# Attention and feed-forward in one kernel: later adding transfers for the second batch, and a new plan that keeps VectorE's two-operand SBUF work behind GpSimd's queue

## The chip, the core and the metric

The kernel runs on one core of a Trainium2 chip. A core has TensorE (PE, matmuls), VectorE (DVE), ScalarE (ACT), GpSimd (POOL) and SyncE (SP, which issues most transfers). Each engine works through its own list of instructions in order, and semaphores tie the lists together. The metric is device time in microseconds (us), the median of several runs.

## The reference, cut to what matters

```python
B, C, H, W = 4, 128, 384, 32          # q: (4, 12288, 128), kv: (4, 384, 32, 128)
kv_pool = kv.reshape(B, H // 4, 4, W // 4, 4, C).mean(axis=(2, 4))   # 768 keys for each batch
k = v = kv_pool.reshape(B, -1, C) @ w_sr
s = (q @ k.transpose(0, 2, 1)) / sqrt(C)
a = exp(s - s.max(-1)); a /= a.sum(-1) + 1e-09
x = (a @ v).reshape(4 * 12288, C)
h = x @ w_in                           # w_in: (128, 2048)
out = (h - tanh(h)) @ w_out            # w_out: (2048, 128)
```

## The kernel before, in words

The 49,152 tokens are cut into 96 groups of 512, 24 for each batch. A group has an attention part and a feed-forward part, and both use expansions about a mean instead of the exact functions. The attention part makes three score tiles of 128x1024 (`big`, L1063), a ScalarE function of them (`p`, L1067), their square on GpSimd (`r2`, shown as r, L1070), a sum over values on TensorE (`x`, L1113), and some 128x512 steps on the side: `qr` (L1048), `m` (L1091), `ql` (L1107) and `dr` (L1120) on GpSimd, `dy` (L1103) and `dl` (L1117) on VectorE. The feed-forward part makes eight hidden tiles (`big`, L1170), squares them on ScalarE (`u`, L1174), forms a cubic term on VectorE (`r`, L1177, a ring of four buffers), multiplies it back into one PSUM bank (`acc`, L1189), and VectorE adds a column and writes the result `o` (L1200).

Before the groups of a batch can run, its keys and weights have to be made. For the first batch this is the prologue. SP loads w_in in four pieces (L412), the first batch's kv in twelve (L566), then w_out in four (L414). `words_of` turns each piece of a weight matrix into float32: two ScalarE steps (L430, L446), three VectorE steps (L433, L436, L440), and a last VectorE step `add` (L449), which adds two SBUF operands. VectorE sums eight of the kv pieces (L580) and GpSimd folds the other four (L574). TensorE turns w_in (L476), multiplies it with itself (L495), and makes keys and values (L644, L632, L649, L677). From the w_in pieces and the centre of the keys come `first` (L756), a chain of small VectorE operations (`first_chain`), and then the batch's own weights: `winr` (L928 and L935) and `Wr` (`by_third`, L970, on GpSimd, one for each quarter, which reads that quarter of w_out). TensorE sums `Wg` against each quarter of w_out into the bank `acc` (`slopes`, L957), and a short chain (L966, L989, L992, L996, L999) ends in the tables that every group of the batch needs. Since `acc` is one bank, no group can begin its sum in it before this chain is over.

Each later batch is pooled by transfers: SP issues a first one (L535), and GpSimd then issues seven that add into the same tile `kvp` (L533), each behind the landing of the one before; `join` adds the two halves.

What sets the order: nothing is written in program order. Each piece of work is a `plan.op` with a step (its place), an engine, a cost, a delay after it (`late`) and, for two-operand VectorE work in SBUF, `port=True`. `Plan.run` walks these with a simple model of the engines, of one port that GpSimd and such VectorE work share, and of the transfer queues. At each turn it takes, on each engine, the lowest step among what can begin soon, and then the engine that begins first. The instructions are emitted in that order. The table MOVES shifts the steps of named pieces; from the fourth group on, each group's steps are the same. BUFS gives the buffers of each ring.

Of the kernel before, what the change touches and what calls it, by code (L numbers as in the profile page):

```python
# [46 lines left out]
class Plan:  # L47
# [36 lines left out]
    def run(self, between):  # L84
# [67 lines left out]
        while True:  # L152
            best = None
            for e, q in ready.items():
                if q:
                    starts = []
                    for r, i in q:
                        held = free.get("port", 0.0) if self.ops[i][5] else 0.0
                        starts.append((max(free.get(e, 0.0), r, held), self.ops[i][0], i, r))
                    soon = min(starts)[0] + self.SOON  # L160
                    step, i, start, r = min((p, i, t, r) for t, p, i, r in starts if t <= soon)
                    if best is None or (start, step, i) < best[:3]:
                        best = start, step, i, e, r
            done = landed(best[0] if best else math.inf)
# [37 lines left out]
def attention_then_ffn(ctx: ExitStack, tc: tile.TileContext, q, kv_by_key, kv_by_place, w_sr, w_in,  # L202
# [17 lines left out]
    plan = Plan(tc)  # L220

    MOVES = {
# [1269 lines left out]
```

## Time and profile before

| | |
|---|---|
| median of 3 runs | 1270.63 us (1270.61 to 1271.1) |
| the profiled execution: time, span | 1270.95 us, 1269.2 us |
| mean granted TensorE clock | 0.988 |
| TensorE busy | 1217.5 us (96%) |
| VectorE, ScalarE, GpSimd busy | 1153.5, 1143.2, 1057.7 us |

The span runs from the first to the last instruction of the profiled execution; the time holds a little more around it. A granted clock of 1.0 is 2.4 GHz, 0.5 is 1.2 GHz. In the rows of a timeline the first number is the start in us from the span's start, the second the length, and the brackets at the end give the idle time of that engine just before and who ended it. Records of neighbouring instructions on one engine can overlap a little.

### The profile page before, as it was taken

What the parts mean: (1) busy time and instruction counts of PE and PEld (TensorE: products, weight loads), DVE (VectorE), ACT (ScalarE), POOL (GpSimd) and SP (SyncE); (2) the same over time, 40 slices, a digit from 0 to 9 for tenths busy, and PEclk for the clock granted to TensorE, in tenths of its full rate; (3) what the DMA queues carried; (4) which work ended last, traced back from release to release, by engine and by line L of the source; (5) the groups of instructions that cost most, each with busy time, mean ns of one, the idle gap of its engine ahead of it and who ended that gap; (6) DMA issues with size and microseconds to landing.
All of it is one profiled execution on the core that took longest, in us unless ns stands there. A gap on an engine that the chain in (4) does not pass through costs nothing.

```text
span 1269.2 us, 16667 instructions
## 1 busy us (share of the span) xinstructions
PE 1217.5 (96%) x5252; PEld 936.1 (74%) x5252; DVE 1153.5 (91%) x1218; ACT 1143.2 (90%) x1373; POOL 1057.7 (83%) x836
## 2 busy tenths in 40 slices
PE   5779999999999999999999999999999999999997
PEld 5656777777777777767777777777777777777775
DVE  6768999999999999998999999998899999999997
ACT  3658999999999999989999999999999999999994
POOL 5668888799999888789999888789988887888881
PEclk9879999999999999999999999999999999999998
DMA  9444111121453111111464111111111111111101
GB/s 358 100 83 92 51 42 42 43 84 59 93 119 89 50 42 42 42 46 56 113 122 106 42 51 42 42 43 59 51 51 42 43 50 42 42 42 51 34 26 35
DMA packets 41713, 84.49 MB, mean 67 GB/s; under 512 B 5040, under 2 KB 7216, under 8 KB 41616
## 3 DMA queue, kind: packets, MB, share of 16 engines
q1 hardware_dynamic: 35904, 66.82, 15.7%
q0 software_dynamic: 5712, 16.52, 7.7%
q8 instruction: 44, 0.72, 0.2%
q14 instruction: 53, 0.43, 0.1%
HBM read 57.93 MB, written 25.39 MB: 66 GB/s over the span
## 4 chain that ended last, share of the span: by engine, by line
PE 84%; DVE 5%; ACT 3%; POOL 2%; issue 2%; DMA 2%; SPq 0%; ACTq 0%; DVEq 0%
PE big L1170 27%; PE acc L1189 25%; PE big L1063 10%; PE x L1113 9%; PE acc L1156 5%; DVE r L1177 3%; PE x L1085 2%; ACT u L1174 2%; PE x L1094 2%; PE acc L1160 2%; PE x L957 1%; ACT p L1067 1%; DMA Wr<-in_kv_by_key_dram 1%; DMA r<-in_kv_by_key_dram 1%; POOL r L1070 1%
## 5 line engine op out<-in xcount | busy, mean ns | idle before, releaser
L1177 DVE SCALAR_TENSOR_TENSOR r<-big,u 128x1024 fp32r<-128x1024 f32 x768 | 902.2, 1219 | 86.4 <-ACT u L1174 64.9
L1174 ACT ACTIVATE u<-big 128x1024 f32<-128x1024 f32 x768 | 762.2, 1028 | 48.5 <-PE big L1170 44.7
L1070 POOL TENSOR_TENSOR r<-p 128x1024 fp32r<-128x1024 f32 x288 | 556.7, 1936 | 111.3 <-ACT p L1067 111.1
L1170 PE MATMUL big<-dr,winr 128*128 128x512 f32 x1536 | 488.1, 407 | 4.2 <-ACT p L1067 2.3
L1189 PE MATMUL acc<-r,Wr 128*128 128x512 f32 x1536 | 454.2, 396 | 2.1 <-DVE o L1200 1.8
L1170 PEld LDWEIGHTS big<-dr,winr 128*128 128x128 f32 x1536 | 271.1, 189 | 105.3 <-DVE r L1177 29.9
L1189 PEld LDWEIGHTS acc<-r,Wr 128*128 128x128 f32 x1536 | 289.0, 189 | 68.9 <-DVE o L1200 2.2
L1067 ACT ACTIVATE p<-big 128x1024 f32<-128x1024 f32 x288 | 296.6, 1030 | 18.9 <-PE big L1063 5.3
L1063 PE MATMUL big<-qr,kTr 128*128 128x512 f32 x576 | 186.8, 406 | 1.5 <-ACT p L1067 0.7
L1113 PE MATMUL x<-r,vvr 128*128 128x512 f32 x576 | 165.0, 394 | 0.2 <-DVE dy L1103 0.2
L1120 POOL TENSOR_TENSOR dr<-dl,yk 128x512 fp32r<-128x512 f32 x96 | 129.3, 1347 | 41.9 <-DVE dl L1117 41.8
L1063 PEld LDWEIGHTS big<-qr,kTr 128*128 128x128 f32 x576 | 101.4, 189 | 41.3 <-ACT p L1067 21.6
L1091 POOL TENSOR_TENSOR m<-yk,q 128x512 fp32r<-128x512 f32 x96 | 129.9, 1353 | 0.0
L1107 POOL TENSOR_TENSOR ql<-q,qr 128x512 fp32r<-128x512 f32 x96 | 129.7, 1352 | 0.0
L1113 PEld LDWEIGHTS x<-r,vvr 128*128 128x128 f32 x576 | 107.5, 188 | 25.4 <-DVE dy L1103 0.9
L1200 DVE TENSOR_SCALAR o<-acc,At 128x512 f32<-128x512 f32 x96 | 71.3, 743 | 1.6 <-PE acc L1160 1.5
L1103 DVE SCALAR_TENSOR_TENSOR dy<-x,yk 128x512 f32<-128x512 f32 x96 | 65.4, 681 | 4.2 <-ACT t L1097 4.2
L1088 ACT ACTIVATE yk<-x 128x512 f32<-128x512 f32 x96 | 58.0, 604 | 10.7 <-PE x L1085 9.4
L1117 DVE TENSOR_TENSOR dl<-x,dy 128x512 fp32r<-128x512 f32 x96 | 65.4, 682 | 1.1 <-PE x L1113 0.4
L1048 POOL TENSOR_SCALAR qr<-q 128x512 fp32r<-128x512 f32 x96 | 62.2, 647 | 1.0 <-DMA q<-in_q_dram 0.9
L1156 PE MATMUL acc<-qr,Lh 128*128 128x512 f32 x192 | 60.5, 397 | 1.5 <-DVE o L1200 1.5
L1097 ACT ACTIVATE t<-x 128x512 f32<-128x512 f32 x96 | 57.9, 603 | 2.0 <-PE x L1094 2.0
(195 smaller groups left out, 640.7 us busy)
## 6 DMA issues: line engine op xcount, KB each, us to landing
q<-in_q_dram SPq DMA_DIRECT2D x96, 256.0 KB
out_dram<-o SPq DMA_DIRECT2D x96, 256.0 KB
kvp<-in_kv_by_place_dram POOLq DMA_DIRECT2D x21, 768.0 KB, 7.2
kc<-inverse SPq DMA_DIRECT2D x12, 256.0 KB
kvp<-in_kv_by_place_dram SPq DMA_DIRECT2D x3, 768.0 KB
winr<-in_kv_by_key_dram SPq DMA_DIRECT2D x4, 512.0 KB
r<-in_kv_by_key_dram SPq DMA_DIRECT2D x4, 512.0 KB
Wr<-in_kv_by_key_dram SPq DMA_DIRECT2D x4, 512.0 KB
```

Of the source, the lines that this page charges most:

```text
L1063: PE.matmul(out=half(plan[s], h), lhsT=plan[kTr][:, n * P : (n + 1) * P], rhs=plan[qr], start=True, stop=True)
L1067: A.activation(out=plan[p], in_=plan[s], func=AF.Silu, scale=1.0 / 3)
L1070: PL.tensor_tensor(out=plan[r], in0=plan[p], in1=plan[p], op=ALU.mult)
L1091: PL.tensor_tensor(out=plan[m], in0=plan[yk], in1=plan[qs], op=ALU.mult)
L1107: PL.tensor_tensor(out=plan[ql], in0=plan[qs], in1=plan[qr].bitcast(F32), op=ALU.subtract)
L1113: PE.matmul(out=plan[num], lhsT=plan[vvr][:, n], rhs=half(plan[f"r2.{g}.{k}"], h), start=(start and h == 0), stop=(stop and h == 1))
L1120: PL.tensor_tensor(out=plan[dr], in0=plan[dl].bitcast(F32), in1=plan[yk], op=ALU.add)
L1156: PE.matmul(out=plan[acc], lhsT=x, rhs=plan[y], start=(start and n == 0), stop=(stop and n == 2))
L1170: PE.matmul(out=half(plan[hp], h), lhsT=plan[winr][:, f * P : (f + 1) * P], rhs=plan[dr], start=True, stop=True)
L1174: A.activation(out=plan[u], in_=plan[hp], func=AF.Square)
L1177: V.scalar_tensor_tensor(out=plan[r], in0=plan[hp], scalar=1.0, in1=plan[u], op0=ALU.add, op1=ALU.mult)
L1189: PE.matmul(out=plan[acc], lhsT=plan[Wr][:, 2 * n + h], rhs=half(plan[r], h), start=(start and h == 0), stop=(stop and h == 1))
```

## The change

Four things are edited. The planner gets a rule: when the next piece would be a VectorE operation that needs the port, begins just as the port comes free, and GpSimd has a queued operation that could begin at most 0.12 later, GpSimd's is taken first. The second batch's first pooling transfer (L535) is given a `late` of 30 in the model, so that the adding transfers behind it are planned later. Two other numbers of the model change (`late` of the w_out loads, cost of `first_chain`). And all of MOVES is replaced; its rows tell a reader nothing, and one line of it stands here.

```diff
         while True:
-            best = None
+            best = pool = None
...
+                    if e == "POOL":
+                        pool = start, step, i, e, r
                     if best is None or (start, step, i) < best[:3]:
                         best = start, step, i, e, r
+            if (best and pool and best[3] != "POOL" and self.ops[best[2]][5] and not self.ops[pool[2]][6]
+                    and pool[0] <= best[0] + 0.12 and 0 < free.get("port", 0.0) <= best[0]
+                    and best[0] <= free["port"] + 1e-9):
+                best = pool
...
-        "load.i.0": -3373.262, "words.i.0": -3532.267, "load.i.1": -881.918, "words.i.1": -947.206,
+        "load.i.0": -4159.973, "words.i.0": -2510.035, "load.i.1": -4127.904, "words.i.1":
...
-        plan.op(load_step, "SP", 0.5, load_words, (), (own,), late=2.0 if kind == "i" else 4.5, dma=1.3)
+        plan.op(load_step, "SP", 0.5, load_words, (), (own,), late=2.0 if kind == "i" else 5.5, dma=1.3)
...
-                    late=0.81 if w else 1.0, dma=5.84 if w else 2.2)
+                    late=0.81 if w else 30.0 if b == 1 else 1.0, dma=5.84 if w else 2.2)
...
-            plan.op(known, on, 3.7, first_chain, ((prep, "h"),), ((prep, "t"), (hb, 8), iv, ("stat", b)))
+            plan.op(known, on, 3.4, first_chain, ((prep, "h"),), ((prep, "t"), (hb, 8), iv, ("stat", b)))
```

No instruction is added or taken away; what the chip sees is another order on each engine. Lines of the changed kernel are eight higher. On SP the fourth w_in piece is loaded ahead of all kv pieces. On VectorE five sums of kv pieces stand ahead of the last two `add` of w_in, where two stood, and three of the four w_out pieces are finished before `first_chain`, where one was. The order changes in the prologue, around the second batch's tables, and in a few places of the third and fourth batch.

The first place is GpSimd around the four `Wr` of the first batch (the last three and the first three of a row stand here). Before:

```order
L970 TENSOR_TENSOR Wr<-wout_69,hb 128x512
L1120 TENSOR_TENSOR dr<-dl,yk 128x512
L1070 TENSOR_TENSOR r_570<-p 128x1024
L1091 TENSOR_TENSOR m<-yk,q 128x512
L1070 TENSOR_TENSOR r_576<-p 128x1024
L970 TENSOR_TENSOR Wr<-wout_69,hb 128x512
L533 DMA kvp<-in_kv_by_place_dram 128x2x768
L1003 TENSOR_TENSOR Lh<-L_595,Lh 128x128
```

And in the changed kernel:

```order
L1078 TENSOR_TENSOR r_435<-p 128x1024
L1099 TENSOR_TENSOR m<-yk,q 128x512
L1128 TENSOR_TENSOR dr<-dl,yk 128x512
L978 TENSOR_TENSOR Wr<-wout_69,hb 128x512 x4
L1078 TENSOR_TENSOR r_547<-p 128x1024
L1011 TENSOR_TENSOR Lh<-L_540,Lh 128x128
```

Four operations stood between the third and the fourth `Wr`; now the four stand together, and the adding transfers (L533, now L541) come after all of this.

The second place is TensorE around the last of the four `slopes` (L957, now L965) and the chain behind it. Before:

```order
L1170 MATMUL big<-dr,winr 128x512 x2
L957 MATMUL acc<-Wg,wout_69 128x129 x4
L989 MATMUL acc<-ident,At 128x128
L996 MATMUL acc<-A,Mn 128x128
L1160 MATMUL acc<-dl,Ah 128x512
L1189 MATMUL acc<-r,Wr 128x512 x6
```

And in the changed kernel:

```order
L1178 MATMUL big<-dr,winr 128x512 x6
L516 MATMUL x<-Mn 128x128
L965 MATMUL acc<-Wg,wout_69 128x129 x4
L1121 MATMUL x<-r_435,vvr 128x512 x2
L997 MATMUL acc<-ident,At 128x128
L1071 MATMUL big<-qr,kTr 128x512 x2
L1178 MATMUL big<-dr,winr 128x512 x2
L1004 MATMUL acc<-A,Mn 128x128
L1178 MATMUL big<-dr,winr 128x512 x2
L1071 MATMUL big<-qr,kTr 128x512 x2
L1121 MATMUL x<-r_547,vvr 128x512 x2
L1168 MATMUL acc<-dl,Ah 128x512
```

Three of the first group's eight hidden tiles stand ahead of the last `slopes`, where seven stood, and the steps of the chain have other matmuls between them.

The third place is TensorE up to the first score tiles (L1063, now L1071). Before:

```order
L632 MATMUL big<-kvp,wsr 128x384
L644 MATMUL big<-wsr,kvp 128x128
L623 MATMUL x<-row,wsr 128x1
L644 MATMUL big<-wsr,kvp 128x128
L649 MATMUL big<-wsr,row 128x128 x3
L756 MATMUL acc<-col,win_67 128x64 x4
L649 MATMUL big<-wsr,row 128x128 x3
L756 MATMUL acc<-col,win_67 128x64 x4
L1063 MATMUL big<-qr,kTr 128x512 x2
L677 MATMUL x<-kc 128x128 x6
```

And in the changed kernel:

```order
L764 MATMUL acc<-col,win_67 128x64 x4
L652 MATMUL big<-wsr,kvp 128x128 x2
L657 MATMUL big<-wsr,row 128x128 x6
L640 MATMUL big<-kvp,wsr 128x384
L764 MATMUL acc<-col,win_67 128x64 x8
L685 MATMUL x<-kc 128x128 x6
L1071 MATMUL big<-qr,kTr 128x512 x2
```

The first scores now stand behind a third `first` (L756, now L764) and the moment of the values (L677, now L685).

## Rows read from the trace of the kernel before

**Rows 1.** The page: busy time of each engine, and TensorE's by slices.

```profile
PE 1217.5 (96%) x5252; PEld 936.1 (74%) x5252; DVE 1153.5 (91%) x1218; ACT 1143.2 (90%) x1373; POOL 1057.7 (83%) x836
PE   5779999999999999999999999999999999999997
```

**Rows 2.** Windows: length, busy us and counts by engine, granted clock, DMA share, GB/s.

```profile
37.30:41.90 4.60, 0.01 (x1) 0.01 (x1) 2.20 (x14) 2.61 (x4) 4.60 (x4) 0.81 0.58 86
41.90:47.00 5.10, 5.10 (x17) 4.30 (x18) 3.12 (x10) 2.38 (x6) 4.22 (x3) 0.50 0.54 128
47.00:65.40 18.40, 15.57 (x83) 11.07 (x81) 14.62 (x21) 10.78 (x15) 13.65 (x11) 1.00 0.36 62
65.40:71.80 6.40, 0.01 (x1) 0.01 (x1) 6.33 (x1) 1.69 (x2) 5.78 (x4) 0.66 0.59 112
71.80:81.10 9.30, 8.22 (x23) 6.16 (x24) 2.79 (x3) 1.67 (x6) 3.68 (x4) 0.50 0.50 85
81.10:98.20 17.10, 13.36 (x54) 9.43 (x52) 11.95 (x12) 13.18 (x15) 8.81 (x7) 1.00 0.44 80
98.20:101.60 3.40, 3.14 (x8) 2.50 (x9) 1.33 (x2) 0.60 (x1) 3.20 (x3) 0.50 0.74 142
...
155.20:190.50 35.30, 35.30 (x152) 27.39 (x151) 33.55 (x34) 34.26 (x40) 30.03 (x22) 1.00 0.14 45
```

**Rows 3.** Timeline around the last `add` of w_out, VectorE, GpSimd and TensorE.

```profile
52.60 0.68 DVE L449 CUSTOM_DVE_ANT_0 wout<-wout,o 128x1024 uint16<-128x1024 uint16 x1
...
64.57 1.71 POOL L1120 TENSOR_TENSOR dr<-dl,yk 128x512 fp32r<-128x512 f32 x1
...
65.15 6.58 DVE L449 CUSTOM_DVE_ANT_0 wout<-wout,o 128x1024 uint16<-128x1024 uint16 x1
65.80 2.31 POOL L1070 TENSOR_TENSOR r<-p 128x1024 fp32r<-128x1024 f32 x1
...
68.88 2.30 POOL L1070 TENSOR_TENSOR r<-p 128x1024 fp32r<-128x1024 f32 x1
...
71.79 2.09 PE L957 MATMUL acc<-Wg,wout 128*128 128x129 f32 x8 [6.41 <-DVE wout L449]
```

**Rows 4.** Timeline of what followed on VectorE and TensorE.

```profile
78.31 4.82 DVE L1177 SCALAR_TENSOR_TENSOR r<-big,u 128x1024 fp32r<-128x1024 f32 x4 [6.57 <-PE acc L1189]
...
88.40 0.74 PE L1156 MATMUL acc<-qr,Lh 128*128 128x512 f32 x2 [1.53 <-DVE o L1200]
...
98.46 0.77 PE L1085 MATMUL x<-qr,Mh 128*128 128x512 f32 x1 [2.22 <-DVE dl L1117]
```

**Rows 5.** Timeline of the prologue up to the first group's shares.

```profile
17.87 3.78 PE L476 MATMUL big<-ident,win 128*128 128x128 f32 x16 [3.39 <-DVE win L449]
18.87 1.21 DVE L580 TENSOR_REDUCE kvp<-winr 128x64 f32<-128x1024 f32 x1
...
32.03 0.71 PE L1063 MATMUL big<-qr,kTr 128*128 128x512 f32 x2
...
32.58 1.50 PE L677 MATMUL x<-kc 128*128 128x128 f32 x12
...
34.39 1.00 PE L756 MATMUL acc<-col,win 128*128 128x64 f32 x8
...
41.89 0.80 PE L1094 MATMUL x<-m,share 128*128 128x512 f32 x1 [4.63 <-POOL m L1091]
```

**Rows 6.** Timeline of VectorE: results of the eighth, ninth and tenth group.

```profile
178.75 0.74 DVE L1200 TENSOR_SCALAR o<-acc,At 128x512 f32<-128x512 f32 x1
...
190.55 0.74 DVE L1200 TENSOR_SCALAR o<-acc,At 128x512 f32<-128x512 f32 x1
...
204.11 0.74 DVE L1200 TENSOR_SCALAR o<-acc,At 128x512 f32<-128x512 f32 x1
```

**Rows 7.** An adding transfer on GpSimd, and a later window in which three begin.

```profile
337.82 1.21 POOL L533 DMA_DIRECT2D kvp<-in_kv_by_place_dram  x1
...
360.00:400.00 40.00, 40.00 (x172) 30.85 (x171) 38.06 (x38) 38.88 (x47) 39.07 (x31) 1.00 0.59 119
```

196 rows, old and new, of the table MOVES are left out of this document.

## The prediction

> **What bounds the kernel now.** I read the page first. TensorE is busy for 96% of the span, and its slices read 9 from the fourth on but for the last; only the first three are low [rows 1]. So the bulk is TensorE's, a change of order can win there next to nothing, and what can be won lies in the first 120 us or at the tail. The profiled execution took 1270.95 us, 0.32 above the median, which is far below what I try to tell apart.
>
> Then I cut the prologue into windows at the places where TensorE stops and where its clock changes [rows 2]. In each window two things are lost: time in which TensorE is idle, and half of the time in which it works at a granted clock of 0.50. From the first stop (37.3) to 101.6 this gives:
>
> - 37.3 to 41.9: 4.59 idle. 41.9 to 47.0: 5.10 busy at half clock, so 2.55.
> - 47.0 to 65.4: 18.40 less 15.57, so 2.83 idle.
> - 65.4 to 71.8: 6.39 idle. 71.8 to 81.1: 1.08 idle, and 8.22 busy at half clock, so 4.11.
> - 81.1 to 98.2: 3.74 idle. 98.2 to 101.6: 0.26 idle, and half of 3.14, so 1.57.
>
> Together 27.1 us. By contrast three steady groups from 155.2 to 190.5 fill 35.30 of 35.30 us [rows 2], and a steady group takes 190.55 less 178.75, 11.8 us [rows 6].
>
> The timeline names the cause of the largest stop. The last `add` of w_out begins at 65.15 on VectorE and takes 6.58 us, where the same operation took 0.68 at 52.60 [rows 3]. It has two operands in SBUF. During all of it GpSimd goes from one operation to the next, four of them from 64.57 to 71.18, and VectorE comes in only when GpSimd runs dry: GpSimd's next piece is the fourth `Wr`, which needs the `add`. TensorE's last `slopes` waits 6.41 us for it [rows 3]. What follows is its echo. The one `acc` bank is blocked until the chain behind `slopes` ends, so the four `r` buffers stay full and VectorE stands for another 6.57 us, until 78.31; then it is the late one, and TensorE waits 1.53 us for the result `o` and 2.22 for `dl` [rows 4]. The first stop, 4.63 us for `m` [rows 5], is another matter: `m` stands in a row of GpSimd that is busy for all 4.60 us of that window [rows 2].
>
> **The change part by part.** No instruction is added or removed, so every term is a wait that goes, shrinks, moves or appears.
>
> The stall at `add`. Behind the third `Wr` stood `dr`, `r`, `m`, `r` and only then the fourth; now the four `Wr` stand together. So GpSimd runs dry, if the `add` has not passed by then, right after the third, and the `add` pays its own 0.68. The last `slopes` also stands behind three hidden tiles of the first group, not seven, so that TensorE reaches it before it has run out of other work, and the chain of small matmuls behind it has hidden tiles, scores and values in between. From 65.4 to 81.1 the kernel lost 6.39 + 1.08 + 4.11 = 11.58. I leave 0.5 of it and take 11.1. If the cover fails, that is if GpSimd's row up to the third `Wr` is the late one, TensorE waits for the same `add` at the new place.
>
> The Trainium skill, in "SBUF — State Buffer", section "Who interferes with whom", says that the port shared by VectorE and GpSimd is a lock held for one whole instruction, and that the order of issue decides who blocks. By that rule the `add` would get its turn when the GpSimd operation in front of it ends, at 64.57 + 1.71 = 66.28, after 1.1 us. The trace does not agree: it waited through four [rows 3]. The wait itself was 6.58 less 0.68, 5.9 us; with the rule's 1.1 in its place the stall and this term would be 4.8 smaller; the measured row decides, and the sum goes by it.
>
> The echo, 3.74 + 0.26 + 1.57 = 5.57. It falls if VectorE's cubes are not held up, since the `acc` bank is free earlier. VectorE still has more to do here than in a steady group, so I leave 1.2 and take 4.4. Its bounds are 0 and 5.6.
>
> The first stop, 4.59 + 2.55 = 7.1. In the changed order more TensorE work (the `y` products and the scores of two groups) stands ahead of the first shares, but the score tiles have three buffers, so TensorE then waits for a `p` of ScalarE instead of for `p`, `r` and `m` one after the other. I leave half of the stop, 2.4, and two thirds of the loss at half clock, 1.7: 4.1 remain, and 3.0 are won. Between 0 and 7.1 all is possible.
>
> The small stops from 47.0 to 65.4, 2.83: left as they are.
>
> The later beginning. TensorE's second set of w_in turns began at 17.87, after 3.39 us of waiting for `add` [rows 5]. Now five kv sums of 1.21 stand ahead of those `add`s, not two. At worst this is 3 x 1.21 = 3.6 us later, at best nothing, since the old ones also waited for the port and for the fourth w_in piece, which is now loaded sooner. I charge 2.0. The first scores (32.03 before) come later still, by the moment (1.50) and a `first` (1.00) that now precede them [rows 5]; but that is work moved on a busy TensorE, and costs nothing by itself.
>
> The adding transfers. Seven on GpSimd leave the prologue, where its row is the tight one, and come between later groups, one in each. Their issue takes 1.21 us [rows 7], and in the third batch the same traffic stands beside a TensorE that is busy for 40.00 of 40.00 us, with GpSimd at 39.07 [rows 7]. So I cost them at nothing; what hides them is about 0.9 us of slack in 40, and if that is gone each could add up to its 1.21, 8.5 in all. The second batch's keys are not needed before 24 groups have run (24 x 11.8 = 283 us), and the last adding transfer is issued by about the ninth group, under 190.55 [rows 6].
>
> Later groups. The second batch's value products and some pieces of the third and fourth batch's tables change places. Such a place costs little: the group with the value products takes 204.11 less 190.55, 13.56 us, against 11.8 [rows 6], and that 1.8 is work that only moves to another group. I take a gain of 1.0, with bounds of -1 and 2.
>
> The sum: 11.1 + 4.4 + 3.0 + 0 - 2.0 + 0 + 1.0 = 17.5. From 1270.95 this is 1253.4, and as a median (0.32 less) 1253.1; I say 1253.
>
> **The rivals.**
>
> *The wait moves.* At its new place the last `add` still waits until GpSimd's row runs dry, and TensorE runs out of work there too, for about its old 6.4 us, without the long stretch at half clock. For it: nothing breaks GpSimd's row from the first `r` to the third `Wr`. Against: that row must end before `Wr` in any case, and more work stands ahead of `slopes` in front of it. Time: 1253 + 6.4 = 1259.4.
>
> *GpSimd becomes the bound* while the second batch is pooled. For it: 39.07 of 40 us in the like window. Against: TensorE's 40.00 in the same row. Seven times 1.21: 1253 + 8.5 = 1261.5.
>
> *The late beginning passes through.* If latency, not TensorE, sets the pace from the first scores on, the moved 2.5 us are lost on top: 1253 + 2.5 = 1255.5.
>
> *Slower: the change doesn't do what it says.* The `add` is held as long as before, since GpSimd's row is as dense, and all of the 27.1 us remains, while the first scores come 2.0 + 2.5 us later: 1270.6 + 4.5 = 1275. It decides if the new wait of the `add` is over 6 us and the tiles in front of `slopes` do not cover it. Against it stands the place of the four `Wr`: the row must run dry there.
>
> **How the numbers follow.** Forecast 0.68, the wait moves 0.12, GpSimd 0.06, the late beginning 0.08, slower 0.04, and 0.02 for no change. The forecast's own bounds: if the first stop goes wholly (4.1 more) and the later groups give 1 more, 1248; if the echo and the first stop give nothing, 1260. The range reaches from 1247 to 1260, which takes in the first and third rival and leaves the others out. A measurement here can tell 0.2%, or 2.5 us, from no change: faster by more than that 0.94, within it 0.02, slower 0.04.
>
> **What would show it.** Right: the last `add` of w_out under 1 us, or waiting while TensorE is busy; no window of ten us past 50 with TensorE under 8; no half clock after about 60; the ninth group's result near 174 where it was 190.55 (16.5 earlier, the sum without the later groups); later groups at 11.8 as before. Wrong: a VectorE two-operand operation of several us beside a row of GpSimd operations at another place, groups four to ten slower than 12 us, or the same loss before 60 us as there was before 100.

## The result, and the profile after

| | before | after |
|---|---|---|
| median of 5 runs | 1271.1 us (1270.61 to 1271.39) | 1252.59 us (1249.61 to 1253.02) |
| ratio | | 0.9849, 95% interval 0.9835 to 0.9864 |
| the profiled execution: time, span | 1270.95, 1269.2 us | 1249.61, 1247.9 us |

The change makes the kernel 18.5 us faster, where 17.5 were forecast. The profiled execution of after was the fastest of its five, so the two spans differ by more, 21.3 us. In a later profile of the same kernel the span was 1249.4 us, with the first result 1.6 us later than below.

The page of after: busy time, and TensorE by slices, against [rows 1].

```profile
PE 1208.5 (97%) x5252; PEld 929.5 (74%) x5252; DVE 1147.2 (92%) x1218; ACT 1142.6 (92%) x1373; POOL 1055.6 (85%) x836
...
PE   5899999999999999999999999999999999999997
```

TensorE now reads 9 from the third slice on, but for the last. The results of the first and the third group, on VectorE's timeline, show where the time came from. Before:

```profile
87.60 0.74 DVE L1200 TENSOR_SCALAR o<-acc,At 128x512 f32<-128x512 f32 x1
...
119.18 0.74 DVE L1200 TENSOR_SCALAR o<-acc,At 128x512 f32<-128x512 f32 x1
```

After, with the ninth group's as well:

```profile
71.78 0.74 DVE L1208 TENSOR_SCALAR o<-acc,At 128x512 f32<-128x512 f32 x1
...
101.22 0.74 DVE L1208 TENSOR_SCALAR o<-acc,At 128x512 f32<-128x512 f32 x1
...
172.56 0.74 DVE L1208 TENSOR_SCALAR o<-acc,At 128x512 f32<-128x512 f32 x1
```

The first result comes 15.8 us earlier. From the first to the third it takes 29.4 us where it took 31.6, 2.1 less (from unrounded times). From the third to the end of the span it takes 1146.7 where it took 1150.1, 3.4 less. The ninth group's result, forecast near 174, stands at 172.56.

The prologue in windows, cut where TensorE stops and its clock changes, against [rows 2] (same columns):

```profile
34.86:40.20 5.34, 4.42 (x23) 3.05 (x21) 4.96 (x19) 5.12 (x10) 2.37 (x2) 1.00 0.23 92
40.20:46.20 6.00, 2.58 (x19) 2.33 (x20) 4.26 (x17) 3.71 (x7) 6.00 (x4) 1.00 0.15 44
46.20:49.60 3.40, 3.40 (x13) 2.97 (x13) 1.82 (x2) 0.00 (x0) 1.72 (x2) 0.50 0.00 0
49.60:61.20 11.60, 10.72 (x66) 8.66 (x64) 8.27 (x9) 6.96 (x13) 6.44 (x6) 1.00 0.08 25
61.20:71.80 10.60, 9.70 (x40) 6.92 (x39) 7.70 (x8) 8.25 (x10) 9.32 (x9) 1.00 0.00 0
```

Counted as in the prediction, idle time and half of the busy time at half clock, the first three windows lose 0.92 + 3.42 + 1.70 = 6.0, where the first stop lost 7.1. The last two lose 0.88 + 0.90 = 1.8, where 47.0 to 81.1 lost 2.83 + 11.58 = 14.4.

The last `add` of w_out, on the timeline of VectorE, GpSimd and TensorE, against [rows 3]:

```profile
52.49 3.04 POOL L978 TENSOR_TENSOR Wr<-wout,hb 128x512 fp32r<-128x512 f32 x3
...
54.51 1.56 DVE L457 CUSTOM_DVE_ANT_0 wout<-wout,o 128x1024 uint16<-128x1024 uint16 x1
...
56.15 1.04 POOL L978 TENSOR_TENSOR Wr<-wout,hb 128x512 fp32r<-128x512 f32 x1 [0.62 <-DVE wout L457]
...
56.13 1.16 PE L965 MATMUL acc<-Wg,wout 128*128 128x129 f32 x8 [0.43 <-DVE wout L457]
```

It waits for the rest of the third `Wr` (to 55.53) and passes: 1.56 us, not 6.58, and TensorE waits 0.43, not 6.41.

The prologue on TensorE up to the first shares and the stop behind them, against [rows 5]:

```profile
19.51 0.80 PE L484 MATMUL big<-ident,win 128*128 128x128 f32 x2 [7.08 <-DVE win L457]
...
34.86 0.71 PE L1071 MATMUL big<-qr,kTr 128*128 128x512 f32 x2
...
41.19 0.50 PE L1102 MATMUL x<-m,share 128*128 128x512 f32 x1 [1.03 <-POOL m L1099]
...
45.05 1.13 PE L965 MATMUL acc<-Wg,wout 128*128 128x129 f32 x8 [2.43 <-DVE hb L888]
```

The second set of turns starts 1.64 us later, the first scores 2.8 later, and the stop for `m` is 1.03 where it was 4.63. Behind it comes a stop of 2.43 for VectorE's `hb`.

### The profile page after: what moved, and what is told of

Same layout as the page of the kernel before. It is cut to its first block, busy times and chain, and to the rows that moved or that the text cites. A ratio compares the mean times of both kernels' runs of the same rounds, so it can differ in the third digit from the quotient of the medians.

```text
span 1247.9 us, 16674 instructions
## 1 busy us (share of the span) xinstructions
PE 1208.5 (97%) x5252; PEld 929.5 (74%) x5252; DVE 1147.2 (92%) x1218; ACT 1142.6 (92%) x1373; POOL 1055.6 (85%) x836
## 4 chain that ended last, share of the span: by engine, by line
PE 80%; POOL 7%; DVE 5%; ACT 3%; issue 2%; DMA 2%; SPq 0%; DVEq 0%; ACTq 0%
PE big L1178 26%; PE acc L1197 24%; PE big L1071 9%; PE x L1121 9%; PE acc L1164 5%; POOL r L1078 3%; DVE r L1185 2%; PE x L1093 2%; PE x L1102 2%; PE acc L1168 1%; ACT u L1182 1%; ACT p L1075 1%; DMA winr<-in_kv_by_key_dram 1%; POOL dr L1128 1%; PE x L965 1%
## 5 line engine op out<-in xcount | busy, mean ns | idle before, releaser
L1078 POOL TENSOR_TENSOR r<-p 128x1024 fp32r<-128x1024 f32 x288 | 562.9, 1961 | 107.9 <-ACT p L1075 107.5
L1075 ACT ACTIVATE p<-big 128x1024 f32<-128x1024 f32 x288 | 296.6, 1030 | 14.7 <-POOL r L1078 3.2
L1071 PE MATMUL big<-qr,kTr 128*128 128x512 f32 x576 | 185.7, 404 | 1.7 <-ACT p L1075 1.7
L1071 PEld LDWEIGHTS big<-qr,kTr 128*128 128x128 f32 x576 | 100.9, 188 | 40.9 <-ACT p L1075 22.5
L1056 POOL TENSOR_SCALAR qr<-q 128x512 fp32r<-128x512 f32 x96 | 65.8, 686 | 0.9 <-DMA q<-in_q_dram 0.7
```

The costliest lines, as they stand in the source:

```text
L1071: PE.matmul(out=half(plan[s], h), lhsT=plan[kTr][:, n * P : (n + 1) * P], rhs=plan[qr], start=True, stop=True)
L1075: A.activation(out=plan[p], in_=plan[s], func=AF.Silu, scale=1.0 / 3)
L1078: PL.tensor_tensor(out=plan[r], in0=plan[p], in1=plan[p], op=ALU.mult)
```

## The experiments

Each run stands beside runs of the kernel before on the same chip, whose median was 1271.26, 1270.86 and 1270.74 us in the three sets. Times are medians, ratios are to before with 95% intervals.

**One operand in the last add.** In the order of before, the last `add` of w_out becomes an operation of the same length that reads one SBUF operand:

```diff
+            if kind == "o" and n == 3:
+                of = rest().rearrange("p (k e) -> p k e", e=8)
+                V.tensor_reduce(out=to[:, 0 : WN // 8], in_=of, op=ALU.add, axis=AX.X)
+                return
```

> The order of before, but the last add of w_out is a reduction of about the same length that reads one SBUF operand instead of two (it leaves out the lower bits of the last quarter of w_out). Theory (the add waited 5.9 us for the port behind GpSimd's row): it takes 0.7 us or less at about 65, TensorE's 6.41 us stop nearly goes, with most of the half-clock stretch and the echo; 1258 to 1264 us, 1260 the likeliest. Rival (the wait is on a semaphore or on data, or the stop is covered elsewhere): the operation still ends at about 71.7, 1270 to 1271 us.

Measured: 1264.05 us, ratio 0.9945 (0.9928 to 0.9961), 7.2 faster. VectorE and TensorE at that place:

```profile
64.67 0.68 DVE L451 TENSOR_REDUCE wout<-o 128x64 f32<-128x512 f32 x1
...
65.40 1.16 PE L961 MATMUL acc<-Wg,wout 128*128 128x129 f32 x8 [0.51 <-DVE wout L451]
...
79.91 0.73 PE L1160 MATMUL acc<-qr,Lh 128*128 128x512 f32 x2 [1.53 <-DVE o L1204]
...
90.83 0.55 PE L1089 MATMUL x<-qr,Mh 128*128 128x512 f32 x1 [2.22 <-DVE dl L1121]
```

The second operand in SBUF is what is held. But the stops for `o` and `dl`, 1.53 and 2.22 us, are those of [rows 4] to the hundredth, though the stall ahead of them is gone: they are no echo of it.

**The fourth `Wr` ahead.** The order of before, with edges in the planner that put the fourth `Wr` ahead of the r, m, r in front of it:

```diff
...
+    plan.after = [("third.0.3", x) for x in ("beyond.2.1", "along.2", "beyond.2.0")]
     plan.run(skip_is_likely)
```

> The order of before with one edge more: the fourth Wr must stand ahead of the r, m, r that stood in front of it on GpSimd. Theory: GpSimd runs dry one operation after the third Wr, the add waits 1 to 2 us instead of 5.9, TensorE's stop falls to about 1.6 us, and the half clock and the echo behind it mostly go: 1259 to 1266 us, 1262 the likeliest. Rival (the group's own r, m, r, which now come later, are as late for TensorE as the add was): 1269 to 1273 us.

Measured: 1262.97 us, ratio 0.9936 (0.9919 to 0.9953), 8.3 faster; the `add` took 1.69 us, and TensorE waited for it:

```profile
66.11 1.16 PE L960 MATMUL acc<-Wg,wout 128*128 128x129 f32 x8 [1.52 <-DVE wout L452]
```

The place of `Wr` alone cures most of the stall, without the rule and with the transfers where they were.

**The rule alone.** Before, with the planner's new rule and nothing else of the change.

> Before with the planner's new rule alone, old table and old costs. The last two Wr stand together on GpSimd in its order. Theory (the dense row of GpSimd is the cause, and the rule makes the planner see it): the 6.4 us stop goes, the late start and the new table's other gains do not come: 1261 to 1267 us. Rival (the gain is the table's): 1269 to 1273 us.

Measured: 1267.7 us, ratio 0.9972 (0.9962 to 0.9983), 3.6 faster, between the two ranges. Every `add` of w_out takes 0.68 or 0.69, but the last two of w_in are put behind all kv sums, and TensorE stands for the second turns:

```profile
28.54 2.08 PE L482 MATMUL big<-ident,win 128*128 128x128 f32 x8 [13.06 <-DVE win L455]
```

**The late beginning alone.** Before, with the one number that the change gives to the second batch's first transfer.

> Before with the late of 30 on the second batch's first transfer alone, so that the adding transfers leave the prologue; the order around the Wr changes with it: two r stand between the third and the fourth Wr, not dr, r, m, r. Theory (transfers cost nothing by themselves, the add waits for what stands in front of the fourth Wr): the add waits about 3 us, the stop halves: 1264 to 1269 us. Rival (the transfers' issues on GpSimd, five of 1.2 us, were what made its row late): 1258 to 1263 us, with the add waiting as long as before.

Measured: 1256.54 us, ratio 0.9885 (0.9868 to 0.9901), 14.7 faster and below both ranges: most of the change's gain from the edit that the prediction had costed at nothing. But with that number the planner also moved other work. So the next three runs move the transfers by themselves: the planner's list is sorted anew after planning, and nothing else changes its place.

**The first transfer alone**, behind the first group's r, m, r, r:

```diff
-        order.sort()
+        g1 = self.names["gather.1.1"]; row = sorted((t, i) for t, i in order if self.ops[i][1] == "POOL" and t > begun[g1]); order = sorted((row[3][0] + 0.001 if i == g1 else t, i) for t, i in order)
...
```

> The order of before with one instruction moved: the second batch's first adding transfer, which stood on GpSimd ahead of the first group's r, m, r, r, now stands behind these four; the other six transfers and every other instruction keep their places. Theory A (the prediction's): the transfers cost nothing where they stand, and the first stop of TensorE (4.63 us for m) is a matter of which shares stand where; no change, 1270 to 1272 us. Theory B: GpSimd stood still at the head of its row, at that transfer (issued at 37.27), while the first p had been ready since about 35.0 (with the transfers moved in the run with the late beginning alone, the first r starts at 34.97 and not at 38.29); then r and m come 3.3 us earlier, the stop falls from 4.63 to about 1.3, and the 6.8 us at half clock behind it go as well, 2.6 to 3.4 more: 1265 us (1263 to 1267), with the add of 6.58 us still there. Theory C: what is won at the first stop is waited for again at the held add, since GpSimd's row up to the fourth Wr has the same length: 1269 to 1271.

Measured: 1268.34 us, ratio 0.9977 (0.9967 to 0.9988), 2.5 faster, in none of the three ranges. The first r starts at 35.61, not at 38.29, and the stop for `m` falls from 4.63 to 1.65. At the last `add` all is as before (the timeline of GpSimd, VectorE and TensorE):

```profile
60.21 1.19 POOL L533 DMA_DIRECT2D kvp<-in_kv_by_place_dram  x1
60.99 1.49 POOL L970 TENSOR_TENSOR Wr<-wout,hb 128x512 fp32r<-128x512 f32 x1
61.99 1.71 POOL L1120 TENSOR_TENSOR dr<-dl,yk 128x512 fp32r<-128x512 f32 x1
63.22 2.32 POOL L1070 TENSOR_TENSOR r<-p 128x1024 fp32r<-128x1024 f32 x1
65.07 1.69 POOL L1091 TENSOR_TENSOR m<-yk,q 128x512 fp32r<-128x512 f32 x1
66.29 2.31 POOL L1070 TENSOR_TENSOR r<-p 128x1024 fp32r<-128x1024 f32 x1
...
62.58 6.59 DVE L449 CUSTOM_DVE_ANT_0 wout<-wout,o 128x1024 uint16<-128x1024 uint16 x1
...
69.22 1.02 PE L957 MATMUL acc<-Wg,wout 128*128 128x129 f32 x3 [6.42 <-DVE wout L449]
```

**The seven transfers alone**, 60 us later: `order = sorted((t + 60.0 * (i in moved), i) for t, i in order)`.

> The order of before with the seven adding transfers of the second batch alone set 60 us later in the order; every other instruction keeps its place, so dr, r, m, r still stand between the third and the fourth Wr. Theory A: the transfers cost nothing, 1270 to 1272. Theory B (they take GpSimd's time in the prologue: 3.3 us of standing at the first, and an issue of about 1.2 us for each of the four before the first result): the first stop goes as in the run that moves one transfer, the add of 6.58 us stays, and 1 to 4 us more go than with one: 1261 to 1265. Theory C: all that the run with the late beginning alone won (14.7 us) is the transfers': 1256 to 1258, and the add is no longer held, because GpSimd reaches the fourth Wr before the words of w_out do.

Measured: 1264.78 us, ratio 0.9949 (0.9932 to 0.9966). The `add` takes 1.12 us here, and the first result comes at 74.8; but the two `join` of the second batch were left ahead of moved transfers (so its keys lack a part), and GpSimd stood there for ones still on the way, 2.72 us at 121.46, with TensorE stopped for 4.28. So the next run takes along what hangs on them.

**The transfers with all that hangs on them**, 55 us later:

```diff
-        order.sort()
+        g = self.names["gather.1.1"]; order = sorted((t + 55.0 * (g <= i < g + 12), i) for t, i in order)
...
```

> The order of before with twelve instructions of the second batch's pooling alone set 55 us later: the seven adding transfers and the two join, the mean and the two copies behind them, so that nothing stands behind a transfer that has not landed; every other instruction keeps its place. (In the run that moved the transfers alone, the two join of the second batch stood ahead of the moved transfers.) Theory C as the runs now bear it out (the transfers lengthen GpSimd's row up to the fourth Wr, and that row is what holds the add and TensorE): what the run of the transfers alone had up to the third result (105.6) without its 7 us at the join: 1264.8 - 7.2 = 1257.6 (1256.5 to 1259). Theory A (the transfers cost nothing and the late beginning worked by the other places that the planner then took): 1264 to 1271.

Measured: 1258.49 us, ratio 0.9907 (0.989 to 0.9923), 12.2 faster, and the first result at 75.5. The same row of GpSimd, in the same order, without the transfer at its head:

```profile
60.53 1.27 POOL L1120 TENSOR_TENSOR dr<-dl,yk 128x512 fp32r<-128x512 f32 x1 [0.60 <-DVE dl L1117]
61.76 2.35 POOL L1070 TENSOR_TENSOR r<-p 128x1024 fp32r<-128x1024 f32 x1
64.07 1.26 POOL L1091 TENSOR_TENSOR m<-yk,q 128x512 fp32r<-128x512 f32 x1
65.30 1.89 POOL L1070 TENSOR_TENSOR r<-p 128x1024 fp32r<-128x1024 f32 x1
67.15 1.03 POOL L970 TENSOR_TENSOR Wr<-wout,hb 128x512 fp32r<-128x512 f32 x1
...
61.24 1.12 DVE L449 CUSTOM_DVE_ANT_0 wout<-wout,o 128x1024 uint16<-128x1024 uint16 x1
...
62.41 0.82 PE L957 MATMUL acc<-Wg,wout 128*128 128x129 f32 x5 [0.95 <-DVE wout L449]
```

GpSimd's row is as dense from `dr` on, and r, m, r still stand ahead of the fourth `Wr`. Yet the `add` passes when `dr` ends at 61.80, and it is r that waits for it (2.35 us, where the next r takes 1.89). So the order of the row does not hold the `add`. Two things are gone: the transfer ahead of the row, and with it the row's unbroken run, since GpSimd now idles 0.60 us before `dr`. An unbroken run by itself does not hold VectorE. In the run of the changed kernel without the rule (below) GpSimd goes r, m, r, r from 37.94 to 45.40 without an idle moment and without a transfer, and a VectorE operation with two SBUF operands, 0.68 us by itself, passes after one r:

```profile
41.27 2.37 DVE L444 SCALAR_TENSOR_TENSOR wout<-Wr,r 128x512 int32<-128x512 int32 x1
```

What is left is the transfer. All seven were moved together; the one directly ahead of the row was not moved alone.

**The changed kernel with the transfers early again** (`late` back at 1.0).

> The changed kernel with one number put back: late of the second batch's first pooling transfer is 1.0 again, not 30, so the planner places the adding transfers in the prologue, the first one again at the head of GpSimd's row, ahead of the first r. The four Wr still stand together and the new table and the rule stay. Theory A (transfers cost nothing): 1252 to 1254. Theory B (the blocked head costs the first stop and its half clock): r starts 2 to 3 us later, and 3 to 7 us are lost against the changed kernel: 1256 to 1260. Theory C (the late beginning is worth in the new table what it was worth in the old, 14.7 us): 1265 to 1268.

Measured: 1251.83 us, ratio 0.9847 (0.9831 to 0.9864): no slower than the changed kernel. The first transfer stands at the head of GpSimd's row again, and r starts at 39.38, not at 37.83. But behind the second transfer the row breaks off before the `add` comes:

```profile
50.84 1.20 POOL L541 DMA_DIRECT2D kvp<-in_kv_by_place_dram  x1
53.00 1.27 POOL L1128 TENSOR_TENSOR dr<-dl,yk 128x512 fp32r<-128x512 f32 x1 [0.97 <-DVE dl L1125]
54.24 3.03 POOL L978 TENSOR_TENSOR Wr<-wout,hb 128x512 fp32r<-128x512 f32 x3
...
57.58 0.68 DVE L457 CUSTOM_DVE_ANT_0 wout<-wout,o 128x1024 uint16<-128x1024 uint16 x1
```

**The changed kernel without the rule.**

> The changed kernel without the planner's new rule; the table, the late beginning and the two other numbers stay. The order then has the two last add of w_in ahead of all sums of kv pieces (they stood behind five), the two last add of w_out behind three Wr, and all four slopes ahead of the first hidden tile. Theory A (the rule only orders the few port operations; the table and the late beginning carry the gain): 1252 to 1254. Theory B (rule and table belong together: with the slopes ahead of all hidden tiles TensorE has no cover while the chain behind them runs): a stop of 3 to 6 us at about 55 to 65 us with half clock behind it, the first result 5 to 8 us later than the 71.8 of the changed kernel, though the turns of w_in come at about 13 and not at 19.5: 1257 to 1261.

Measured: 1259.47 us, ratio 0.9912 (0.9895 to 0.9928), 7 us slower than the changed kernel. With all `slopes` ahead of the first hidden tile TensorE stands twice, and the first result comes at 81.0:

```profile
47.74 1.86 PE L961 MATMUL acc<-Wg,wout 128*128 128x129 f32 x8 [2.59 <-ACT Wg L957]
52.73 1.22 PE L1117 MATMUL x<-r,vvr 128*128 128x512 f32 x2 [3.13 <-DVE dy L1107]
```

**The adds of w_in early.** The changed kernel with one move on VectorE (the rows as they stand after it):

```diff
 L448 SCALAR_TENSOR_TENSOR win_67<-u,r_125 128x512
+L457 ISA win_67<-win_67,o 128x1024 x2
 L588 TENSOR_REDUCE kvp<-winr 128x64
...
-L457 ISA win_67<-win_67,o 128x1024 x2
 L615 TENSOR_REDUCE row<-kvp 128x4 x2
```

> The changed kernel with the two last add of w_in ahead of the first five sums of kv pieces on VectorE, where they stood behind them; every other instruction keeps its place. Theory A (the prediction's: the later beginning costs about 2 us): the second set of turns starts at about 13 and not at 19.5, and the first scores come 1 to 2 us earlier: 1250.5 to 1251.5. Theory B (the first scores hang on the kv sums, which end where they ended, at about 26): the turns come 6 us earlier, TensorE stops later for the sums instead, and nothing is won: 1252 to 1253. Theory C (a two-operand add beside GpSimd's folds is held): the second of the two takes 1.2 us or more, the kv sums end 1 us later: 1253 to 1254.

Measured: 1251.42 us (1251.07 to 1252.46), the changed kernel beside it 1251.87 (1250.6 to 1253.5): no difference that these runs show. The turns start 6 us earlier, and then TensorE stands for the kv sums and works on at half clock:

```profile
13.75 3.78 PE L484 MATMUL big<-ident,win 128*128 128x128 f32 x16 [0.41 <-DVE win L457]
...
25.19 1.62 PE L640 MATMUL big<-kvp,wsr 128*128 128x384 f32 x2 [4.02 <-POOL winr L582]
...
38.15 0.72 PE L1071 MATMUL big<-qr,kTr 128*128 128x512 f32 x2
```

Its window of that stretch: 10.20 us at a granted clock of 0.50.

```profile
24.40:34.60 10.20, 9.41 (x39) 8.84 (x40) 7.75 (x17) 2.87 (x6) 6.59 (x9) 0.50 0.85 283
```

**A searched order, and the changed kernel again.** The first has another order of the first 303 pieces.

> The changed kernel with its first 303 pieces of work written out in another order, found by moving one at a time, so that the first r of GpSimd and the first results come earlier: the adds of w_in first, the copy of the second half of the keys ahead of two steps of w_out on ScalarE, the first qr ahead of the last fold, and the four Wr spread out again (after r, r, m, and an r between the first and the second). If the first 70 us are bound by the order in which small work stands on ScalarE, VectorE and GpSimd: first result at 66 to 69 where the changed kernel had 71.8, and 3 to 5 us less: 1248 to 1250. If a two-operand operation of VectorE is held once more behind GpSimd's row, which such an order can bring about: an add of over 3 us, and 1253 to 1260.

> The changed kernel again, beside the runs that alter it: 1249.6 to 1253.0, as in its first five runs.

Measured: 1252.42 us (1251.1 to 1253.5) and 1251.87 us. The searched order did not do what it was made for: first result at 74.7, with three stretches of 3.4 us at half clock (24.4, 44.9, 51.7). No version here is faster than the changed kernel by more than the spread of its runs. The new table alone, and the two other numbers of the model, were not run by themselves.

## Why the prediction was right in its sum, and which steps were not

**The stall at `add`, 11.1.** Its size was about right: from 47.0 the loss fell from 14.4 to 1.8, 12.6 us. These 12.6 hold the small stops ahead of it too, 2.83, which the prediction had left as they are. Taken away by itself the stall gave less, 7.2 and 8.3: the small stops stay, and behind them, up to the first result, TensorE still stands for 3.1 us in the one run and 3.8 in the other. Its mechanism was half right. The four `Wr` together do cure it (8.3 us by that alone). But "VectorE comes in only when GpSimd runs dry" holds only behind an adding transfer; in the run that moved only the transfers and what hangs on them the `add` passed through the same row after one operation. That is what the rule of the Trainium skill weighed there ("SBUF — State Buffer", section "Who interferes with whom") gives: a turn when the GpSimd operation in front ends. The prediction set it aside on a row behind a transfer, and only such rows break it here.

**The adding transfers, 0: the step that failed.** "So I cost them at nothing" was argued from where they go to. Where they came from was not priced, though the row was tight. In the old order they cost 12.2 us, more than seven issues of 1.21 (8.5): one held up the first r, and with them in place the `add` waited. In the new order they cost nothing that the runs show (1251.83 with them early). There the first r is late once more (39.38), but the `add` comes when GpSimd's row has broken off. So the sum came out by luck in this: nearly the same time had been entered under the place of `Wr` (11.1) and the first stop (3.0), and in the old order either cure ends the stall.

**The echo, 4.4: right in size, wrong in its mechanism.** The stops of 1.5 and 2.2 us stand, within 0.06 us, in all six runs in which the stall is gone and the old table stays. From the first to the third result these take 32.4 (one operand), 31.6 (`Wr` first), 31.5 (rule alone), 30.3 (late alone), 30.9 (transfers alone) and 31.5 us (transfers and joins), before 31.6; the three with the new table, after, early transfers and no rule, take 29.4, 29.2 and 29.2. So the loss goes with the new table (and the two numbers that stand with it in all three), which gives the second and third group other places, and not with the stall. Windows from the first to the third result (columns of [rows 2]), before:

```profile
87.60:119.18 31.58, 28.03 (x109) 20.64 (x109) 23.78 (x24) 25.11 (x30) 25.32 (x19) 0.95 0.43 92
```

and after:

```profile
71.78:101.22 29.44, 28.41 (x114) 20.29 (x115) 25.43 (x26) 27.71 (x33) 28.70 (x20) 1.00 0.48 101
```

Before, 3.55 us are idle there and 3.14 are worked at half clock, so 5.1 are lost; after, 1.0. That is 4.1 less, near the 4.4. In the time only 2.1 of it shows, since five more matmuls stand in this stretch (114, not 109) and five fewer ahead of the first result (286, not 291).

**The first stop, 3.0.** `m` is waited for 1.03 us, but then TensorE waits 2.43 for VectorE's `hb`, and 3.4 us pass at half clock. Of 7.1 lost, 6.0 still are: 1.1 won. In the later profile of the same kernel the half clock lasts 6.8 us at this place:

```profile
43.90:50.70 6.80, 5.14 (x20) 4.88 (x21) 3.18 (x10) 1.97 (x3) 4.53 (x3) 0.50 0.00 0
```

There 6.9 are lost, so that 0.2 to 1.1 are won where 3.0 were forecast.

**The later beginning, -2.0.** It was charged for a delay that is there (1.64 us at the turns), but it is not what sets the first result: with the `add`s put forward nothing was won. TensorE's idle time went from 12.4 to 21.2, and the work behind it ran at half clock, so that the first scores came at 38.15, later than 34.86.

**The later groups, 1.0.** 3.4 measured. Of these 2.4 are two stops, once each around the third and fourth batch's tables: 1.61 us of TensorE waiting for `kc` before, under 0.5 now. The first of them, before:

```profile
557.88 0.47 PE L1085 MATMUL x<-qr,Mh 128*128 128x512 f32 x1 [1.61 <-DVE kc L753]
```

and after:

```profile
539.09 0.47 PE L1093 MATMUL x<-qr,Mh 128*128 128x512 f32 x1 [0.40 <-DVE kc L761]
```

Another 1.1 us lie in the last group, which takes 9.4 us before and 8.2 after: in the profile of before the granted clock is 0.50 from 1255.30 to 1258.71. This is not the change's: the changed kernel with early transfers has that stretch too, and the old order with the first transfer moved has not. So the change gave the later groups about 2.2.

Of the 15.8 us at the first result, 12.6 + 1.1 are the terms of the stall and of the first stop; the other 2.1 I have not split, but the five matmuls that now stand behind that result are in it. Of the rivals, the moved wait, GpSimd as the bound and the slower one did not come; whether the 2.5 us of work moved ahead of the first scores pass through, as the third has it, no run tried by itself.

What brought the gain is not one of the edits. The late beginning gives 14.7 in the old table and nothing in the new one; the rule gives 3.6 in the old and 7 in the new. In the old table either takes the stall at `add` away, so they don't add up there. In the new one the `add` passes without the rule as well (1.10 us), and what comes back without it are TensorE's two stops of 2.59 and 3.13 us, with all `slopes` ahead of the first hidden tile.

## What to carry to other kernels

Before a move is costed at nothing, price the place that the work leaves, not only the one that it goes to. Where a two-operand VectorE operation takes several times its own length, look at what stands ahead of the row that holds it, above all for a DMA issue on GpSimd, and try the cure alone. Take an edit out of the new kernel as well as putting it alone into the old one: where the two numbers differ, the edits depend on each other, and what one edit is worth has no single number.

## What the runs showed of the hardware that was not expected

Behind the issue of an adding transfer GpSimd's records overlap. In the profile of before 65 of the 76 operations that follow such an issue without a gap begin over 0.3 us (0.46 in the median) before the one ahead ends; of the 598 others none does (0.04). An idle moment ends it. Behind the transfer of [rows 7], on GpSimd's timeline of before, ql and r are recorded 0.4 us longer than elsewhere; after 0.23 us of idleness the next r takes 1.90 again:

```profile
338.64 1.72 POOL L1107 TENSOR_TENSOR ql<-q,qr 128x512 fp32r<-128x512 f32 x1
339.90 2.31 POOL L1070 TENSOR_TENSOR r<-p 128x1024 fp32r<-128x1024 f32 x1
342.44 1.90 POOL L1070 TENSOR_TENSOR r<-p 128x1024 fp32r<-128x1024 f32 x1 [0.23 <-ACT p L1067]
```

The pace from start to start is the same, but the record of the next operation begins before the one ahead ends. In all fourteen profiles a VectorE operation that was held in a row without a transfer ahead lost at most 1.7 us, one GpSimd operation; the two that lost 5.9 (before, and with the first transfer moved) stood in such an overlapping row. That the overlap is what keeps VectorE out fits every row, but was not tried by itself.

Also, an idle stretch of TensorE that comes earlier need not be better: 7.08 us idle at 12.4 with the work behind it at a granted clock of 0.91 in the mean (19.50 to 34.86), and 4.02 idle at 21.2 with 10.2 us at half clock behind it, gave the same time.
